# The first pair of heads of a fused attention and mixture kernel: one scaled rope table, keys before queries, queries in two column parts

## The chip, the cores and the metric

The kernel runs on one core of a Trainium2 chip. The metric is the device time of one execution in microseconds (us); less is better. A core has five engines with an instruction queue each: TensorE (PE, with weight loads shown apart as PEld), VectorE (DVE), ScalarE (ACT), GpSimd (POOL) and SyncE (SP), which here issues nearly all DMA transfers. An engine takes its instructions in the order in which they stand in its queue.

## What is computed

Three stages follow each other: attention over 4 batches of 8 heads, a gated layer over the positions, and a second attention with four experts. The change lies at the start of the first stage, whose reference is this:

```
q_rot, k_rot = rotate(q), rotate(k)            # rope: x1*cos - x2*sin, x1*sin + x2*cos
scores = q_rot @ k_rot.T / sqrt(64)            # per head, 576 x 576
attn = exp(scores - max); attn /= sum
out  = attn @ v                                # 576 x 64 per head
```

All of it is float32. Products that need full precision are made of parts: a value x is split into a high part, x rounded to the matmul format fp32r, and a low part, x minus the high part.

## The kernel before

The first stage goes through 16 pairs of heads. Class `Work` holds one pair. Head 0 of a pair lies on partitions 0 to 63 (slice `a`), head 1 on 64 to 127 (slice `c`), head dimension on the partitions, the 576 positions along the columns.

Preparation of a pair: `load` fetches tile t0 (queries) and t1 (keys), 576 KB each; each holds the values and the values with their halves swapped, so rope is two multiplications by the table `rp` and one addition. Then the rotated tiles are split and laid out: `q2` holds the high part of a head's queries on one half of the partitions and the low part on the other; `qz` holds the high part on one half and zeros on the other; `kh` holds the high part of the keys twice, `kl` (tile lo) the low part. In the trace the first pair's tiles stand as t, q, qz, kh and lo. A block of 128 query rows then takes four matmuls, two with q2 and kh, two with qz and kl: high x high, low x high and high x low. For all pairs but the first, `rope` runs on POOL, `parts` makes the high part on DVE and the low part on POOL, and `fill_q` and `fill_k` send them to their places by ten DMAs (144 KB each) within the chip. For the first pair, where all engines wait, `first` and `fill_direct` do it on DVE, ACT and POOL directly: queries first, then keys, whole 576 columns at a time. The table held in memory is scaled by 1/8; ACT makes a second copy times 8 for the keys.

A pair has nine blocks of 128 rows (four and a half of each head). Function `slot(k)` handles block k, and writes into the queues: on ACT the exponential of block k; on PE the scores of block k+1 and the transposes of block k-1; on DVE the row maximum (nmax) of block k+1; after each transposition a copy out of PSUM (g), on ACT for even blocks and on DVE for odd ones; in certain slots a gathering of leftover columns (DVE, e<-e) and the products with v (PE, ps_o). Scores have two PSUM buffers, so the scores of block k+1 wait for the exponential of block k-1. The order on PE, ACT, DVE and POOL within this stage is the written order (`keep_in_program_order`, switched on by `fixed`); on SP only some transfers are held in order, and a scheduler places the rest.

Within the first pair's slots the second pair is prepared: POOL multiplies its tiles by the table, adds those of the queries, and DVE adds those of the keys in slot 3. `parts(0)`, the queries, runs in slot 2, `parts(1)`, the keys, in slot 4.

Before the first pair's scores PE multiplies zeros (64 matmuls written, of several shapes). The zero halves of qz and the zero blocks of q2 are written by ACT at the very start, by `Pair.__init__`: per pair two blocks of q2, and 18 pieces of 64 columns of qz.

Of the kernel before, what the change touches and what calls it, by code (L numbers as in the profile page):

```python
# [43 lines left out]
def fused_kernel(ctx, tc, qk, v, w_in, w_out, w_sg, g_ln, b_sg, wqk, wvg, wo, rope, cst, out):  # L44
# [68 lines left out]
    class Pair:  # L113
# [5 lines left out]
        def __init__(self, one, x, some, turned=False):  # L119
            self.turned = turned  # L120
            self.q2 = one.tile([P, 2, 640], F32R, name=f"q2_{x}")
            self.qz = one.tile([P, 2, S], F32R, name=f"qz_{x}")
            z = slice(0, 64) if turned else slice(512, 576)
            for o in (self.q2[:, 0, 576:640], self.q2[:, 1, z]):
                ACT.activation(o, some[:, 0:64], AF.Copy, scale=0.0)
            for o in (self.qz[64:128, 0], self.qz[0:64, 1]):
                if not turned:
                    i = f(self.q2[0:64, 0, 576:640]).rearrange("p (o n) -> p o n", o=1).to_broadcast([64, 9, 64])
                    nc.sync.dma_start(f(o).rearrange("p (c n) -> p c n", c=9), i)
                    continue  # L130
                for c in range(0, S, 64):
                    ACT.activation(o[:, c:c + 64], some[0:64, 0:64], AF.Copy, scale=0.0)

        def block(self, j, i):

# [19 lines left out]
        def fill_q(self, qh, ql):  # L155
            q2, qz = self.q2, self.qz
            a, c = slice(0, 64), slice(64, 128)
            todo = [(q2[a, 0, 0:S], qh[a, :]), (qz[a, 0], qh[a, :])]
            if self.turned:
                todo += [(q2[c, 1, 64:640], qh[c, :]), (qz[c, 1], qh[c, :]), (q2[a, 1, 64:640], ql[c, :])]  # L160
            else:
                todo += [(q2[c, 1, 0:512], qh[c, 0:512]), (qz[c, 1, 64:S], qh[c, 0:512]), (q2[a, 1, 0:512], ql[c, 0:512])]
            todo.append((q2[c, 0, 0:S], ql[a, :]))
            if not self.turned:
                for o, i in ((q2[c, 1, 576:640], qh[c, 512:576]), (q2[a, 1, 576:640], ql[c, 512:576]),
                             (qz[c, 1, 0:64], qh[c, 512:576])):
# [4 lines left out]
        def fill_direct(self, pool, q, k, kl):  # L171

            q2, qz = self.q2, self.qz
            kh = self.kh = pool.tile([P, 2, S], F32R, tag="kh", name="kh", bufs=2)
            self.kl = kl
            a, c = slice(0, 64), slice(64, 128)

            def low(o, x, h):
                DVE.tensor_tensor(o, x, f(h), op=ALU.subtract)

            ACT.copy(q2[a, 0, 0:S], q[a, :])
            low(q2[c, 0, 0:S], q[a, :], q2[a, 0, 0:S])
            ACT.copy(kh[a, 0, :], k[a, :])
            DVE.tensor_copy(kh[c, 0, :], k[a, :])
            low(kl[a, :], k[a, :], kh[a, 0, :])
            ACT.copy(qz[a, 0], q[a, :])
            ACT.copy(q2[c, 1, 64:640], q[c, :])
            low(q2[a, 1, 64:640], q[c, :], q2[c, 1, 64:640])
            ACT.copy(kh[c, 1, :], k[c, :])
            DVE.tensor_copy(kh[a, 1, :], k[c, :])  # L190
            low(kl[c, :], k[c, :], kh[c, 1, :])
            nc.sync.dma_start(f(qz[c, 1]), f(q2[c, 1, 64:640]))

    def factor_out(wk, t, d):
        rr = wk.tile([9, P], F32, tag="rr", name="rr", bufs=1)
# [150 lines left out]
    with ExitStack() as st:  # L346
# [6 lines left out]
        ld2 = st.enter_context(tc.tile_pool(name="a_ld2", bufs=2))  # L353
        wk = st.enter_context(tc.tile_pool(name="a_wk", bufs=2))
        ptp = st.enter_context(tc.tile_pool(name="a_pt", bufs=1))
        rp = one.tile([P, 2, 2, S], F32, name="rp")
        zero = one.tile([P, P], F32, name="zero")
        DVE.memset(zero, 0.0)
        prs = [Pair(opd, x, zero, True) for x in range(2)]
# [17 lines left out]
        class Work:  # L377
# [3 lines left out]
            def load(self, n):  # L381
                self.n, self.b, self.p, self.pr = n, n // NP, n % NP, prs[n % 2]
                self.ts = []
                for x in range(2):
                    t = ld.tile([P, 2, S], F32, tag=f"t{x}", name=f"t{x}")
                    d = nc.sync.dma_start(t, qk[self.b, self.p, :, x])
                    if n == 1 and x == 0:
                        tc.keep_in_program_order(d)
                    if n == 0 and x == 0:
                        nc.sync.dma_start(rp[:, 0], rope)  # L390
                        for i in range(2):
                            ACT.activation(rp[:, 1, i], rp[:, 0, i], AF.Copy, scale=8.0)
                    self.ts.append(t)
                if n == 0:
                    nc.sync.dma_start(ident, cst[:, 0:P])

            def load_values(self):
                self.vt = ld.tile([P, NKB, 2, D], F32, tag="v", name="v", bufs=3)
                nc.sync.dma_start(self.vt, v[self.b, self.p])

            def first(self):

                ts = self.ts
                for x, i, eng in ((0, 0, DVE), (1, 1, POOL), (0, 1, DVE), (1, 0, DVE)):
                    eng.tensor_tensor(ts[x][:, i], ts[x][:, i], rp[:, x, i], op=ALU.mult)
                for t in ts:
                    DVE.tensor_tensor(t[:, 0], t[:, 0], t[:, 1], op=ALU.add)
                lo = ld2.tile([P, S], F32R, tag="lo1", name="lo1")
                self.pr.fill_direct(opd, ts[0][:, 0], ts[1][:, 0], lo)

            def rope(self, x, steps=(0, 1, 2), engine=POOL):
                t = self.ts[x]
                for i in steps:
                    if i < 2:
                        engine.tensor_tensor(t[:, i], t[:, i], rp[:, x, i], op=ALU.mult)
                    else:
                        engine.tensor_tensor(t[:, 0], t[:, 0], t[:, 1], op=ALU.add)

            def parts(self, x):
# [5 lines left out]
                POOL.tensor_tensor(lo, t[:, 0], f(hi), op=ALU.subtract)  # L425
# [101 lines left out]
        def slot(k):  # L527
# [97 lines left out]

        works = {0: Work(), 1: Work()}

        warm, warm2 = bank("l"), bank("o")
        zr = wk.tile([P, P], F32R, tag="e", name="zr", bufs=4)
        DVE.tensor_copy(zr, zero)  # L630
        for _ in range(16):
            PE.matmul(warm[:, 0:P], zero, zero, start=True, stop=True)
        for i in range(8):
            for h in (slice(0, 64), slice(64, 128)):
                PE.matmul(warm[h, 0:P], zero[:, 0:64], zero, start=True, stop=True)
        for i in range(8):
            for o, h in ((warm, slice(0, 64)), (warm2, slice(64, 128))):
                PE.matmul(o[:, 0:P], zero[h], zero[h], start=True, stop=True)
        for i in range(8):
            for o, h in ((warm, slice(0, 64)), (warm2, slice(64, 128))):  # L640
                PE.matmul(o[:, 0:P], zr[h], zr[h], start=True, stop=True)
        works[0].load(0)
        works[0].load_values()
        works[0].first()
        works[1].load(1)
        fixed[0] = True
        works[1].rope(0)
        works[1].load_values()
        works[1].rope(1, (0, 1))
        works[0].start()  # L650
        works[0].scores(0)
        works[0].maxima(0)
# [2 lines left out]
        for k in range(9 * B * NP + 7):  # L655
            n, x = divmod(k, 9)
            slot(k)
            if x in W_AT[4 if n == NP * B - 1 else min(n, 2 + n % 2)]:
                next(wload, None)
            if k == 9 * 4:  # L660
# [758 lines left out]
def layouts(q, k, v, moe_w_in, moe_g_ln, moe_w_sg, moe_b_sg, moe_w_out,  # L1419
# [16 lines left out]
    def chunks(w):  # L1436
# [60 lines left out]
```

## Time and profile before

| | us |
|---|---|
| median of 3 runs | 685.34 (685.2 to 685.43) |
| the profiled execution | 685.67 |
| its span, first to last instruction | 683.9 |
| PE busy | 669.8 (98%) |
| DVE busy | 453.8 (66%) |
| ACT busy | 428.7 (63%) |
| POOL busy | 343.5 (50%) |

The difference between the profiled execution's time and its span, 1.8 us, lies before the first and after the last instruction. Times in rows are us from the start of the span unless marked ns. Nearly all instructions carry line L58, that of a helper that records every operation, so rows are told apart by engine and tiles.

### The profile page before, as it was taken

The page shows a single profiled execution, that of the slowest core. Times are in us where ns is not written, and L with a number is a line of the kernel's source. Part 1 is how long each engine was busy: PE and PEld are TensorE (multiplying, and loading weights), DVE is VectorE, ACT ScalarE, POOL GpSimd, SP SyncE. Part 2 cuts the span into 40 slices and gives each one's busy share as a digit, 9 for nine tenths or more (in the row PEclk, how much of TensorE's full clock was granted, in tenths as well). Part 3 has the DMA queues.
Part 4 walks back from the last instruction along what each step waited for, and adds up shares of the span by engine and source line. Part 5 has one row for each costly group of instructions (what it writes and reads, how often), then busy time and mean ns, then how long its engine had stood idle before and what let it go on. Part 6 is the DMA issues. An engine that isn't in the chain of part 4 may idle for free.

```text
span 683.9 us, 13699 instructions
## 1 busy us (share of the span) xinstructions
PE 669.8 (98%) x4781; PEld 588.2 (86%) x4781; DVE 453.8 (66%) x1026; ACT 428.7 (63%) x1050; POOL 343.5 (50%) x333
## 2 busy tenths in 40 slices
PE   6999999999999999999999999999999999999997
PEld 6777777777777777799999999999999989999985
DVE  5777777777777867478964764664247666556673
ACT  6577776767777777564472473472156676666674
POOL 1886777778888861562446227206223443342320
PEclk9799999999999999999999999999999999999999
DMA  8588887888788762652465233055455364443522
GB/s 301 162 252 255 233 257 203 245 242 255 222 238 256 224 179 84 184 160 79 117 186 176 87 118 119 17 139 158 126 163 142 92 171 103 124 134 77 139 83 77
DMA packets 65538, 112.47 MB, mean 164 GB/s; under 512 B 20527, under 2 KB 25726, under 8 KB 65470
## 3 DMA queue, kind: packets, MB, share of 16 engines
q1 hardware_dynamic: 62734, 105.92, 53.6%
q10 hardware_dynamic: 2736, 5.68, 2.8%
q8 instruction: 38, 0.62, 0.4%
q14 instruction: 30, 0.25, 0.1%
HBM read 58.32 MB, written 18.98 MB: 113 GB/s over the span
## 4 chain that ended last, share of the span: by engine, by line
PE 89%; DVE 5%; ACT 4%; issue 1%; DMA 1%; SPq 0%; ACTq 0%; DVEq 0%
PE ps_S L58 48%; PE ps_o L58 17%; PE ps_t L58 14%; PE ps_f L58 5%; PE ps_s L58 3%; PE ps_l L58 2%; DVE nmax L58 1%; ACT qz L58 1%; ACT e L58 1%; DVE ga L58 1%; DMA x<-yd 1%; ACT ga L58 0%; ACT vh L58 0%; DVE g L58 0%; DVE q L58 0%
## 5 line engine op out<-in xcount | busy, mean ns | idle before, releaser
L58 ACT ACTIVATE e<-ps_S,nmax 128x576 f32<-128x576 f32 x144 | 108.0, 750 | 70.7 <-DVE nmax L58 70.1
L58 DVE TENSOR_REDUCE nmax<-ps_S 128x1 f32<-128x576 f32 x144 | 108.7, 755 | 58.0 <-PE ps_S L58 55.7
L58 PE MATMUL ps_t<-ident,e 128*128 128x128 f32 x776 | 122.0, 275 | 1.2 <-ACT e L58 0.7
L58 PEld LDWEIGHTS ps_t<-ident,e 128*128 128x128 f32 x776 | 95.8, 141 | 5.4 <-ACT e L58 1.3
L58 POOL TENSOR_TENSOR t<-t,rp 128x576 f32<-128x576 f32 x61 | 85.4, 1422 | 15.0 <-ACT rp L58 9.2
L58 PE MATMUL ps_S<-kh,q 128*128 128x288 f32 x352 | 88.0, 343 | 4.7 <-ACT kh L58 2.9
L58 PEld LDWEIGHTS ps_S<-kh,q 128*128 128x128 f32 x352 | 54.5, 193 | 33.3 <-issue 10.2
L58 PE MATMUL ps_o<-g,v 128*64 128x320 f32 (+1 forms) x512 | 76.2, 418 | 0.0
L58 POOL TENSOR_TENSOR lo<-t,hi 128x576 fp32r<-128x576 f32 x30 | 43.2, 1440 | 49.0 <-DVE hi L58 49.0
L58 PE MATMUL ps_S<-lo,qz 128*128 128x288 f32 x304 | 66.5, 300 | 1.4 <-DVE lo L58 1.4
L58 PEld LDWEIGHTS ps_o<-g,v 128*64 128x64 f32 x512 | 31.3, 136 | 24.2 <-issue 9.5
L58 PE MATMUL ps_S<-yh,w 128*128 128x288 f32 x256 | 51.8, 304 | 0.0
L58 PEld LDWEIGHTS ps_S<-lo,qz 128*128 128x128 f32 x304 | 49.8, 193 | 1.7 <-DVE lo L58 1.7
L58 ACT ACTIVATE e<-e,nmax 128x128 f32<-128x128 f32 (+4 forms) x72 | 42.2, 586 | 13.6 <-DVE nmax L58 13.4
L58 POOL TENSOR_TENSOR yl<-x,yh 128x640 fp32r<-128x640 f32 x16 | 26.0, 1630 | 47.7 <-ACT yh L58 47.7
L58 ACT COPY g<-ps_t 128x512 f32<-128x512 f32 x80 | 46.7, 584 | 3.0 <-PE ps_t L58 2.4
L58 DVE COPY g<-ps_t 128x512 f32<-128x512 f32 x64 | 43.6, 681 | 1.4 <-PE ps_t L58 1.3
L58 POOL TENSOR_TENSOR t<-t 128x576 f32<-128x576 f32 x29 | 41.4, 1427 | 2.3
L58 PEld LDWEIGHTS ps_S<-yh,w 128*128 128x128 f32 x256 | 38.7, 189 | 0.0
L58 ACT ACTIVATE ga<-ga 128x512 f32<-128x512 f32 (+1 forms) x34 | 22.3, 656 | 25.5 <-DVE ga L58 25.5
L58 PE MATMUL ps_S<-wsh,vh 128*128 128x288 f32 x160 | 34.6, 297 | 0.8 <-DVE u L58 0.5
L58 POOL TENSOR_TENSOR gxl<-u,gxh 128x576 fp32r<-128x576 f32 x16 | 22.8, 1434 | 24.0 <-ACT gxh L58 24.0
(290 smaller groups left out, 1751.3 us busy)
## 6 DMA issues: line engine op xcount, KB each, us to landing
t<-in_qk_dram SPq DMA_DIRECT2D x32, 576.0 KB
kh<-hi SPq DMA_DIRECT2D x92, 144.0 KB
q<-hi SPq DMA_DIRECT2D x38, 144.0 KB
qz<-hi SPq DMA_DIRECT2D x38, 144.0 KB
q<-lo SPq DMA_DIRECT2D x38, 144.0 KB
v<-in_v_dram SPq DMA_DIRECT2D x16, 320.0 KB
sa<-xr SPq DMA_DIRECT2D x16, 288.0 KB
xd<-sa SPq DMA_DIRECT2D x16, 288.0 KB
```

What stands on the lines that cost most here:

```text
L58: ins = op(*a, **k)
```

## The change

- `rp` holds one table, scaled by 1/sqrt(8) for queries and keys alike; ACT's copy of it goes. It is loaded in two transfers of 288 KB, one per factor.
- The first transfers are keys, table, queries (before: queries, table, keys). More transfers are held in written order on SP.
- `fill_direct` goes. `first` now ropes the keys on DVE, then the first 320 columns of the queries on DVE; ACT casts keys and these query columns; the low part of the second head's 320 columns is made on POOL. The other 256 columns are roped on POOL, and split in slot 1: two casts on ACT, two subtractions on DVE, and two DMAs of 64 KB for their copies in qz.
- The second pair: keys are multiplied first and split in slot 3 (before 4); queries are added on DVE in slot 4 and split in slot 5 (before 2), with their low part on DVE (before on POOL).
- `fill_q` sends the low part of the first head third instead of last, for all pairs.
- PE's zero matmuls before the scores become 18 of one shape, and three more stand behind the scores of slots 0, 1 and 2.
- The zeros of qz are written by two ACT instructions of 576 columns per pair instead of 18 of 64.

```diff
-                for c in range(0, S, 64):
-                    ACT.activation(o[:, c:c + 64], some[0:64, 0:64], AF.Copy, scale=0.0)
+                i = some[0:64, 0:64].rearrange("p (o n) -> p o n", o=1).to_broadcast([64, 9, 64])
+                ACT.activation(o.rearrange("p (c n) -> p c n", c=9), i, AF.Copy, scale=0.0)
...
-            todo = [(q2[a, 0, 0:S], qh[a, :]), (qz[a, 0], qh[a, :])]
+            todo = [(q2[a, 0, 0:S], qh[a, :]), (qz[a, 0], qh[a, :]), (q2[c, 0, 0:S], ql[a, :])]
...
-            todo.append((q2[c, 0, 0:S], ql[a, :]))
...
-        rp = one.tile([P, 2, 2, S], F32, name="rp")
+        rp = one.tile([P, 2, S], F32, name="rp")
...
+                for x in (1, 0) if n < 2 else (0, 1):
+                    d = nc.sync.dma_start(self.ts[x], qk[self.b, self.p, :, x])
+                    if n < 2:
                         tc.keep_in_program_order(d)
-                    if n == 0 and x == 0:
-                        nc.sync.dma_start(rp[:, 0], rope)
+                    if n == 0 and x == 1:
                         for i in range(2):
-                            ACT.activation(rp[:, 1, i], rp[:, 0, i], AF.Copy, scale=8.0)
+                            tc.keep_in_program_order(nc.sync.dma_start(rp[:, i], rope[:, i]))
...
+                full, s, u = slice(0, S), slice(0, 320), slice(320, S)
+                s1, u1 = slice(64, 384), slice(384, 640)
+                roped(k, full)
+                k = k[:, 0]
+                ACT.copy(kh[a, 0], k[a])
+                ACT.copy(kh[c, 0], k[a])
+                roped(w, s)
+                hi = one.tile([P, S], F32R, tag="hi1", name="hi1")
+                DVE.tensor_copy(hi, k)
+                low(kl, k, hi)
+                ACT.copy(q2[a, 0, s], q[a, s])
+                low(q2[c, 0, s], q[a, s], q2[a, 0, s])
+                ACT.copy(qz[a, 0, s], q[a, s])
+                ACT.copy(kh[c, 1], k[c])
+                ACT.copy(q2[c, 1, s1], q[c, s])
+                low(q2[a, 1, s1], q[c, s], q2[c, 1, s1], POOL)
+                ACT.copy(kh[a, 1], k[c])
+                ACT.copy(qz[c, 1, s], q[c, s])
+                roped(w, u, POOL)
+                yield
+                for o, i in ((q2[a, 0, u], q[a, u]), (q2[c, 1, u1], q[c, u])):
+                    ACT.copy(o, i)
+                low(q2[c, 0, u], q[a, u], q2[a, 0, u])
+                low(q2[a, 1, u1], q[c, u], q2[c, 1, u1])
+                for o, i in ((qz[a, 0, u], q2[a, 0, u]), (qz[c, 1, u], q2[c, 1, u1])):
+                    tc.keep_in_program_order(nc.sync.dma_start(f(o), f(i)))
+                yield
...
-                if x == (2 if n == 0 else 1):
-                    nx.parts(0)
-                if x == (4 if n == 0 else 3):
+                if n == 0 and x == 4:
+                    nx.rope(0, (2,), DVE)
+                if x == (5 if n == 0 else 1):
+                    nx.parts(0, POOL if n else DVE)
+                if x == 3:
                     nx.parts(1)
...
+            if k == 1:
+                next(start)
+            if k < 3:
+                warmed(3)
...
-    rope = np.stack([C / 8, Sg / 8], 1).astype(np.float32)
+    rope = (np.stack([C, Sg], 1).astype(np.float64) / np.sqrt(8.0)).astype(np.float32)
```

DVE at the start of the program, from the first multiplication to the last low part of the first pair. Before, t_266 is the queries and t_271 the keys:

```order
L58 TENSOR_TENSOR t_266<-t_266,rp 128x576 x2
L58 TENSOR_TENSOR t_266<-t_266 128x576
L58 TENSOR_TENSOR t_271<-t_271,rp 128x576
L58 TENSOR_TENSOR q_0_150<-t_266,q_0_150 64x576
L58 TENSOR_TENSOR t_271<-t_271 128x576
L58 TENSOR_TENSOR q_0_150<-t_266,q_0_150 64x576
L58 CAST kh<-t_271 64x576 x2
L58 TENSOR_TENSOR lo_282<-t_271,kh 64x576 x2
```

The same place after the change, where t_186 is the keys and t_185 the queries:

```order
L58 TENSOR_TENSOR t_186<-t_186,rp 128x576 x2
L58 TENSOR_TENSOR t_186<-t_186 128x576
L58 TENSOR_TENSOR t_185<-t_185,rp 128x320 x2
L58 TENSOR_TENSOR t_185<-t_185 128x320
L58 CAST hi_204<-t_186 128x576
L58 TENSOR_TENSOR lo_195<-t_186,hi_204 128x576
L58 TENSOR_TENSOR q_0_150<-t_185,q_0_150 64x320
```

The keys come first, their low part is one instruction on 128 partitions instead of two on 64, and the queries have 320 columns.

DVE in the first pair's slots, from the gathering of slot 1 to the second pair's last split. Before, hi_352 belongs to the second pair's queries, t_298 and hi_398 to its keys:

```order
L58 TENSOR_REDUCE e<-e 128x64
L58 TENSOR_REDUCE nmax<-ps_S 128x1
L58 COPY g_194<-ps_t 128x4x128
L58 CAST hi_352<-t_296 128x576
L58 TENSOR_REDUCE nmax<-ps_S 128x1
L58 TENSOR_REDUCE e<-e 128x64
L58 TENSOR_TENSOR t_298<-t_298 128x576
L58 TENSOR_REDUCE nmax<-ps_S 128x1
L58 COPY g_194<-ps_t 128x4x128
L58 CAST hi_398<-t_298 128x576
```

After it, t_219 and hi_304 are the second pair's keys, t_218, hi_358 and lo_359 its queries:

```order
L58 TENSOR_TENSOR q_0_150<-t_185,q_0_150 64x256 x2
L58 TENSOR_REDUCE nmax<-ps_S 128x1
L58 COPY g_162<-ps_t 128x4x128
L58 TENSOR_REDUCE nmax<-ps_S 128x1
L58 TENSOR_REDUCE e<-e 128x64
L58 TENSOR_TENSOR t_219<-t_219 128x576
L58 CAST hi_304<-t_219 128x576
L58 TENSOR_REDUCE nmax<-ps_S 128x1
L58 COPY g_162<-ps_t 128x4x128
L58 TENSOR_TENSOR t_218<-t_218 128x576
L58 TENSOR_REDUCE nmax<-ps_S 128x1
L58 TENSOR_REDUCE e<-e 128x64
```

Two subtractions of the first pair now stand in front of the fourth maximum, an addition and (right behind the last row shown) a cast and a subtraction of the second pair's queries behind it.

PE from the zero matmuls to the fourth block, after the change:

```order
L58 MATMUL ps_l<-zero 128x128 x18
L58 MATMUL ps_S<-kh,q_0_150 128x288 x2
L58 MATMUL ps_S<-lo_195,qz_151 128x288 x2
L58 MATMUL ps_S<-kh,q_0_150 128x288 x2
L58 MATMUL ps_S<-lo_195,qz_151 128x288 x2
L58 MATMUL ps_l<-zero 128x128 x3
L58 MATMUL ps_S<-kh,q_0_150 128x288 x2
L58 MATMUL ps_S<-lo_195,qz_151 128x288 x2
L58 MATMUL ps_t<-ident,e 128x128 x4
L58 MATMUL ps_l<-zero 128x128 x3
```

Before, the zero matmuls ended with 16 of tile zr, and from the first scores on the same rows stood without the groups of three.

## Rows read from the trace of the kernel before

**Rows 1.** The page: span, and busy time of each engine with its share

```profile
span 683.9 us, 13699 instructions
PE 669.8 (98%) x4781; PEld 588.2 (86%) x4781; DVE 453.8 (66%) x1026; ACT 428.7 (63%) x1050; POOL 343.5 (50%) x333
```

**Rows 2.** Windows: stretch, length, busy PE PEld DVE ACT POOL, PEclk, DMA share, GB/s

```profile
32.10:45.90 13.80, 13.80 (x104) 10.89 (x103) 10.16 (x21) 9.75 (x27) 12.40 (x10) 1.00 0.84 246
```

**Rows 3.** Windows, PE alone: stretch, length, PE busy, PEclk, DMA share, GB/s

```profile
3.00:10.00 7.00, 7.00 (x91) 1.00 1.02 405
11.00:13.00 2.00, 0.00 (x0) 1.00 0.65 233
14.00:15.00 1.00, 0.52 (x2) 0.58 0.68 147
18.00:24.00 6.00, 5.56 (x25) 0.50 0.16 68
24.00:25.00 1.00, 1.00 (x9) 0.80 0.00 0
```

**Rows 4.** Timeline, first pair's preparation: start, us, engine, operation [idle before <-releaser]

```profile
1.05 7.39 PE L58 MATMUL ps_l<-zero 128*128 128x128 f32 x65 [1.05 <-DVE zero L58]
5.60 2.86 ACT L58 ACTIVATE qz<-zero 64x64 fp32r<-64x64 f32 x18
5.93 1.43 DVE L58 TENSOR_TENSOR t<-t,rp 128x576 f32<-128x576 f32 x2 [4.68 <-DMA rp<-in_rope_dram]
9.51 0.66 ACT L58 CAST q<-t 64x576 fp32r<-64x576 f32 x1
13.91 0.60 PE L58 MATMUL ps_S<-kh,q 128*128 128x288 f32 x2 [2.94 <-ACT kh L58]
15.88 0.85 PE L58 MATMUL ps_S<-lo,qz 128*128 128x288 f32 x2 [1.36 <-DVE lo L58]
```

**Rows 5.** Timeline of the first pair's blocks, and the second pair's first two

```profile
18.44 0.85 PE L58 MATMUL ps_S<-kh,q 128*128 128x288 f32 x2 [0.75 <-ACT e L58]
22.47 0.69 DVE L58 COPY g<-ps_t 128x512 f32<-128x512 f32 x1
27.48 0.45 DVE L58 CAST hi<-t 128x576 fp32r<-128x576 f32 x1
32.12 0.53 PE L58 MATMUL ps_S<-kh,q 128*128 128x288 f32 x2
33.44 0.61 PE L58 MATMUL ps_S<-kh,q 128*128 128x288 f32 x2
```

**Rows 6.** Lines by form, of ACT until 100 us and of POOL: busy, mean ns

```profile
L58 ACT COPY xt<-ps_o 128x320 f32<-128x320 f32 x4 | 1.7, 419 | 0.0
L58 POOL TENSOR_TENSOR zl<-xt,zh 128x320 fp32r<-128x320 f32 x7 | 6.2, 882 | 0.6
```

**Rows 7.** Timeline, DVE beside POOL in the first pair

```profile
24.11 0.74 DVE L58 TENSOR_REDUCE nmax<-ps_S 128x1 f32<-128x576 f32 x1
24.26 1.41 POOL L58 TENSOR_TENSOR lo<-t,hi 128x576 fp32r<-128x576 f32 x1 [0.40 <-DVE hi L58]
24.77 0.20 DVE L58 TENSOR_REDUCE e<-e 128x64 f32<-128x64 f32 x1
24.90 1.39 DVE L58 TENSOR_TENSOR t<-t 128x576 f32<-128x576 f32 x1
```

**Rows 8.** Timeline, DVE beside POOL in the second stage

```profile
409.00 0.68 DVE L58 TENSOR_TENSOR vl<-gv,vh 128x512 fp32r<-128x512 f32 x1
...
409.34 1.64 POOL L58 TENSOR_TENSOR xl<-sa,xh 128x576 fp32r<-128x576 f32 x1 [0.51 <-DMA sa<-xr]
...
409.72 1.81 DVE L58 TENSOR_TENSOR vh<-g,vh 64x512 fp32r<-64x512 f32 x1
```

**Rows 9.** Timeline, SP: issue of the second pair's last four transfers

```profile
28.29 2.46 SPq L153 DMA_DIRECT2D kh<-hi  x4
```

**Rows 10.** DMA view from 24.2 to 32.8, in 40 slices of 0.215 us

```profile
GB/s 0 0 0 0 0 161 214 214 231 193 193 225 300 246 86 96 246 193 193 290 171 204 300 225 193 279 171 193 236 204 225 290 279 204 225 214 247 215 43 129
```

More of the change, by code (lines that the diff above doesn't have):

```diff
@@ L169, in fill_q @@
                 nc.sync.dma_start(f(o), f(i))
[L171 to L192, printed above, removed]
     def factor_out(wk, t, d):
@@ L384, in load @@
                 for x in range(2):
-                    t = ld.tile([P, 2, S], F32, tag=f"t{x}", name=f"t{x}")
-                    d = nc.sync.dma_start(t, qk[self.b, self.p, :, x])
-                    if n == 1 and x == 0:
+                    self.ts.append(ld.tile([P, 2, S], F32, tag=f"t{x}", name=f"t{x}"))
+                for x in (1, 0) if n < 2 else (0, 1):
+                    d = nc.sync.dma_start(self.ts[x], qk[self.b, self.p, :, x])
+                    if n < 2:
                         tc.keep_in_program_order(d)
-                    if n == 0 and x == 0:
-                        nc.sync.dma_start(rp[:, 0], rope)
+                    if n == 0 and x == 1:
@@ L391, in load @@
                         for i in range(2):
-                            ACT.activation(rp[:, 1, i], rp[:, 0, i], AF.Copy, scale=8.0)
-                    self.ts.append(t)
+                            tc.keep_in_program_order(nc.sync.dma_start(rp[:, i], rope[:, i]))
                 if n == 0:
-                    nc.sync.dma_start(ident, cst[:, 0:P])
+                    tc.keep_in_program_order(nc.sync.dma_start(ident, cst[:, 0:P]))
             def load_values(self):
                 self.vt = ld.tile([P, NKB, 2, D], F32, tag="v", name="v", bufs=3)
-                nc.sync.dma_start(self.vt, v[self.b, self.p])
+                tc.keep_in_program_order(nc.sync.dma_start(self.vt, v[self.b, self.p]))
@@ L401, in first @@
             def first(self):
[L403 to L409, printed above, removed]
+                pr, (q, k) = self.pr, self.ts
@@ new lines, in first, with roped @@
+                q2, qz, a, c = pr.q2, pr.qz, slice(0, 64), slice(64, 128)
+                kh = pr.kh = opd.tile([P, 2, S], F32R, tag="kh", name="kh", bufs=2)
+                kl = pr.kl = ld2.tile([P, S], F32R, tag="lo1", name="lo1")
+                def roped(t, s, engine=DVE):
+                    for i in range(2):
+                        engine.tensor_tensor(t[:, i, s], t[:, i, s], rp[:, i, s], op=ALU.mult)
+                    engine.tensor_tensor(t[:, 0, s], t[:, 0, s], t[:, 1, s], op=ALU.add)
@@ new lines, in low @@
+                def low(o, x, h, engine=DVE):
+                    engine.tensor_tensor(o, x, f(h), op=ALU.subtract)
+                q, w = q[:, 0], q
+                full, s, u = slice(0, S), slice(0, 320), slice(320, S)
[6 more added lines that the diff above has]
+                hi = one.tile([P, S], F32R, tag="hi1", name="hi1")
@@ L414, in rope, with parts @@
                     if i < 2:
-                        engine.tensor_tensor(t[:, i], t[:, i], rp[:, x, i], op=ALU.mult)
+                        engine.tensor_tensor(t[:, i], t[:, i], rp[:, i], op=ALU.mult)
                     else:
                         engine.tensor_tensor(t[:, 0], t[:, 0], t[:, 1], op=ALU.add)
-            def parts(self, x):
+            def parts(self, x, engine=POOL):
                 t = self.ts[x]
@@ L424, in parts @@
                 DVE.tensor_copy(hi, t[:, 0])
-                POOL.tensor_tensor(lo, t[:, 0], f(hi), op=ALU.subtract)
+                engine.tensor_tensor(lo, t[:, 0], f(hi), op=ALU.subtract)
                 if x == 0:
@@ L626, in fused_kernel, with warmed @@
         works = {0: Work(), 1: Work()}
[L628 to L641, printed above, removed]
+        warm = bank("l")
+        def warmed(n):
+            for _ in range(n):
+                PE.matmul(warm[:, 0:P], zero, zero, start=True, stop=True)
+        fixed[0] = True
+        warmed(18)
         works[0].load(0)
         works[0].load_values()
-        works[0].first()
+        start = works[0].first()
+        next(start)
         works[1].load(1)
-        fixed[0] = True
-        works[1].rope(0)
+        works[1].rope(1, (0, 1))
         works[1].load_values()
-        works[1].rope(1, (0, 1))
+        works[1].rope(0, (0, 1))
         works[0].start()
@@ L657, in fused_kernel @@
             slot(k)
+            if k == 1:
+                next(start)
+            if k < 3:
+                warmed(3)
             if x in W_AT[4 if n == NP * B - 1 else min(n, 2 + n % 2)]:
```

## The prediction

> **What bounds the kernel now.** I read the page first, then busy time by windows, then the timeline of the first 34 us. The page shows PE busy for 669.8 of 683.9 us [rows 1], so almost all of the span is PE working through its queue. From the second pair on this is exact: between 32.1 and 45.9 PE is busy for 13.80 of 13.80 us [rows 2]. A change in the first pair is therefore worth what it moves the moment from which PE never waits again. I take as that mark the scores of the second pair's second block, at 33.44 [rows 5]: up to there the change moves instructions, and behind it the queues of PE, ACT and DVE are the same.
>
> The other 14 us lie mostly ahead of that mark. PE multiplies zeros from 1.05 to 11, stands still from 11 to 13.9, does two score matmuls, and waits until 15.88 for the keys' low part [rows 3, 4]. Its clock follows: full from 11 to 13, a mean of 0.58 between 14 and 15, and 0.50 (1.2 GHz) from 18 to 24, where PE is busy for 5.56 of 6 us; then a mean of 0.80 between 24 and 25 [rows 3]. So it fell after PE had stood still, and came back only after it had worked nearly without gaps. Two score matmuls take 0.85 us at 1.2 GHz and 0.53 us at 2.4 [rows 5].
>
> **The preparation of the first pair.** In the trace the first multiplication starts at 5.93, when the table has landed behind the queries, 1,152 KB in all [rows 4]. Between 3 and 10 the DMA engines move 405 GB/s [rows 3], so 576 KB take 1.46 us and half a table 0.73. With the keys and the table's first half in front, DVE starts at 5.2, has its second factor at 5.93, and after two more operations of 0.72 us the rotated keys at 7.5 (0.72 is half of the 1.43 for two [rows 4]). The queries land one transfer later than the table, at 7.3 to 7.4. A 320-column operation with two inputs on DVE has no row. It costs between 0.20 (64 columns [rows 7]) and 0.72; I take 0.48, by a straight line between them, and three end at 8.9. The keys' high part costs 0.45 [rows 5], their low part 0.72, the queries' low part 0.48: DVE is through at 10.5. Both bounds move this by at most 1.1 us (four operations, 0.28 each).
>
> ACT first writes zeros. A wide copy has no row of its own; the nearest, a cast of 64x576, takes 0.66 [rows 4], so 2 of them replace 2.86 us per pair, ACT is free at 5.3 instead of 8.5, and even at twice the price the keys at 7.5 find it idle. Also the 1.2 us of copying the table go. Then come eight casts: four of 576 columns at 0.66, four of 320 at 0.42 (the row of the same width from PSUM [rows 6]). They follow each other with 0.1 of overlap, with a pause for the queries at 8.9, and end at 11.8. On POOL the second head's low part waits for the sixth cast, at 10.7, and takes 0.88 [rows 6], to 11.6. So the first block's scores start at 10.5 (before: 13.91, and 15.88 for the second half), the second's at 11.7.
>
> **The clock and the zero matmuls.** A zero matmul is two instructions; 65 of them filled 7.39 us [rows 4], so 36 end between 5 and 6.7. PE then stands still until 10.5, for 3.8 us or more where before it was 2.9, so I let the clock fall about when the scores begin. Scores at 1.2 GHz (1.1 to 1.2 us a block with its second half) and three zero matmuls (6 x 0.21 = 1.3 us at that clock) then keep PE busy almost without gap from 10.5 to 14.2. Before came to such a stretch only late, since PE was busy for just 0.52 of the microsecond from 14 to 15. I let the clock come back at 14.2; the bounds are that it never falls and that it takes as long as before, some ten microseconds. The third block's scores start at 14.0, 0.8 later than without the group of zeros in front; the other two groups cost 0.7 each at 2.4 GHz and stand where PE would wait for ACT or for the DMA of the last columns, so they cost nothing. That cover goes if the clock stays low.
>
> **From 14 to the mark it is DVE that sets the time.** The two subtractions of the first pair's last 256 columns (0.41 each, the same line) can start at 16.2, after the transposes and casts of slot 1. POOL is then multiplying the second pair's tiles without pause, 1.41 us an instruction [rows 7]. The trace shows what that does: an addition on DVE took 1.39 instead of 0.72 because POOL's subtraction from 24.26 to 25.67 had to end first [rows 7], while nmax, which reads PSUM, kept its 0.74. And at 409.00 [rows 8] the two take turns: DVE's subtraction makes POOL's take 1.64, and DVE's next one waits for all of that, 1.81 for an operation of 0.68. So of two in a row the second loses about 1.1. The second subtraction ends at 18.2 instead of 17.1, and the fourth block's maximum starts there. Behind it stand four maxima (0.66 apart, as from 24.11 to 24.77), two copies of 0.69, two gatherings (0.13), two additions (0.72), two casts (0.45) and the queries' subtraction (0.72): 7.0 us, overlaps of some 0.1 each taken off one and handovers put on the other. POOL is at work on the third pair's tiles by then, since their loads are long there, and the last cast and subtraction again wait, 0.3 and 1.0: the queries' low part is there at 26.7. In before POOL made it, beside DVE.
>
> The Trainium skill, page "SBUF — State Buffer", states in the passage with the single rule on ports that a two-input DVE instruction in SBUF and a reading POOL instruction exclude each other for a whole instruction, by order of issue. The trace agrees (1.81 against 0.68). Counted without this rule, the sum would come out 2.1 us earlier.
>
> Then SP sends six transfers for the queries. In the trace four issues take 2.46 us, 0.62 each [rows 9]; from 24.21, the issue of the first, bytes flow from 25.3 on and ten transfers are through at 32.3 to 32.7 [rows 10], that is 2.2 to 2.6 us behind the last one's issue at 30.1. With 2.4, the third lands at 29.2 and the sixth, issued at 28.7, at 31.1. The second pair's first two blocks start then, where PE with its transposes and products would have come by 27.6 and 29. For before the same walk gives 33.1 for the mark where the trace has 33.4, so I add the same 0.3: 31.4 against 33.4, a gain of 2.0 us.
>
> **The sum.** Start of scores 3.4 us earlier for the first half and 5.4 for the whole block; given back: about 0.8 by zero matmuls at the low clock, 2.1 by POOL and DVE in turns, and the wait for the queries' transfers. It stands against the profiled execution: 685.67 (span 683.9 and 1.8 around it) less 2.0 is 683.7. The median of the runs shown is 0.3 below that execution, so 683.3. The rest moves nothing on the mark: `fill_q`'s new order delays three transfers by one place in pairs that have some 10 us until they are needed, and the first load of the second stage's weights comes later but before its use in the second pair.
>
> **Rivals.**
> 1. The clock stays at 1.2 GHz beyond 14.2. Then the second and third groups of zeros take 1.3 instead of 0.7 each and stand ahead of scores that are ready. Until 17.6 that costs 1.4 at the mark, until 21 2.1. Time 684.7 to 685.4. For it: before it took ten microseconds to come back. Against: there PE had wide gaps at first, here it has none of that size. Chance 0.25.
> 2. The clock does not fall, or DVE and POOL miss each other at 16.2: 0.4 to 1.0 less, 682.3 to 682.9. For it: 0.1 us decides who gets the turn. Against: PE stands still for longer than before. Chance 0.15.
> 3. The queries' transfers replace the gain. They are queued behind the keys' four and a load of 576 KB (1.46 us), and a missed turn of DVE adds 1.4. Two such shifts together put the mark at 33.4 to 34: 685 to 685.8. Against: the load's place is 1 us ahead of the first query transfer. Chance 0.10.
> 4. Slower: the wait for the queries itself stops PE from 27.6 to 29.2 and again to 31, its work between them short, and the clock falls again with the second pair. Before's fall lasted from about 14.2 to 24.4; 10 us at half rate in a stretch where PE is never idle cost 5 us, half of that 2.5 if it returns sooner. 685.8 to 688.4, taken at 688. It decides if PE stands still as it did from 11 to 13.9. The Trainium skill, page "TensorE: Matmul & The Clock Gate", section "HAM oscillation — how this bites in real kernels", describes waits for transfers that put the clock back each time. Only the one fall of before shows it here. Against: the pieces of waiting are 1.6 and 0.7. Chance 0.08.
>
> **How the numbers follow.** The walk has 0.42. Its own range, from the bounds of the 320-column operations and of the landing, is 682.8 to 684.2. Rivals 1 to 3 widen it to 682.2 and 685.5, which leaves out rival 4 and the outer ends of the others, 0.2. A difference of 0.2%, 1.4 us, is about what a measurement of this kernel can tell from none, so faster means below 684.0. Most of the walk and rival 2 lie there, 0.54; the walk's late end, rival 1 and rival 3 are within, 0.38; above 686.7 most of rival 4, 0.08.
>
> **What would show it.** In the changed profile: the keys' multiplication at 5.2 and the first scores at 10.5, with two wide zero copies; PEclk at 0.50 only from about 11 to 14; DVE's subtraction on the queries' second part, and the second pair's, taking 1.4 to 1.8; the second pair's first scores near 29.5 with PE idle before them, and the second block's near 31.4. It is wrong if PEclk stays at 0.50 beyond 17, if PE reaches the second pair without waiting, or if the mark moves by 2 us and the end does not.

## The result, and the profile after

The changed kernel takes 692.35 us (median of 4 runs, 691.1 to 693.08), the kernel before 685.38 beside it: a ratio of 1.0102, 95% interval 1.009 to 1.0114. Forecast were 683.3 and a range of 682.2 to 685.5. The profiled execution took 693.08 us with a span of 691.3, 7.4 more than before [rows 1].

The page of the changed kernel: PE is busy for 1.6 us more [rows 1] and stands still for 5.8 us more (19.9 of 691.3 against 14.1 of 683.9).

```profile
span 691.3 us, 13548 instructions
PE 671.4 (97%) x4723; PEld 588.8 (85%) x4723; DVE 457.3 (66%) x1027; ACT 427.4 (62%) x1021; POOL 342.9 (50%) x334
```

The first pair's preparation came out nearly as walked through; compare [rows 4]. Timeline of the changed kernel (start us, us, engine, operation, idle before and its releaser):

```profile
2.44 1.38 ACT L58 ACTIVATE qz<-zero 64x576 fp32r<-64x576 f32 x2
...
5.57 1.43 DVE L58 TENSOR_TENSOR t<-t,rp 128x576 f32<-128x576 f32 x2 [4.57 <-DMA rp<-in_rope_dram]
...
8.96 0.49 DVE L58 TENSOR_TENSOR t<-t 128x320 f32<-128x320 f32 x1
...
11.19 0.54 PE L58 MATMUL ps_S<-kh,q 128*128 128x288 f32 x2 [3.67 <-DVE q L58]
...
17.32 3.23 DVE L58 TENSOR_TENSOR q<-t,q 64x256 fp32r<-64x256 f32 x2 [0.56 <-ACT q L58]
...
23.92 2.83 SPq L153 DMA_DIRECT2D kh<-hi  x4
...
26.85 0.53 SPq L363 DMA_DIRECT2D t<-in_qk_dram  x1
27.61 1.86 DVE L58 TENSOR_TENSOR lo<-t,hi 128x576 fp32r<-128x576 f32 x1
...
29.50 0.46 SPq L168 DMA_DIRECT2D q<-lo  x1
...
33.81 0.82 PE L58 MATMUL ps_S<-kh,q 128*128 128x288 f32 x2 [3.16 <-issue]
...
36.26 1.04 PE L58 MATMUL ps_S<-kh,q 128*128 128x288 f32 x2
```

First scores 2.7 us earlier than before; but the second pair's low part is made at 29.47 (forecast 26.7), its transfer is issued at 29.50, and PE, idle for 3.16 us, starts that pair at 33.81 instead of 32.12 [rows 5]. The view names no releaser for that wait ("issue"); by the semaphore steps of the trace the low part had landed at 33.61. The mark is at 36.26, 2.8 later than before. Windows of PE for the stretches of [rows 3] and two more (length, PE busy, PEclk, DMA share, GB/s):

```profile
11.00:13.00 2.00, 1.45 (x7) 0.87 0.32 126
14.00:15.00 1.00, 1.00 (x7) 0.50 1.01 387
16.00:18.00 2.00, 2.00 (x20) 1.00 0.04 14
18.00:24.00 6.00, 3.74 (x25) 0.89 0.44 123
24.00:25.00 1.00, 1.00 (x6) 0.50 0.00 0
30.00:34.00 4.00, 0.84 (x8) 0.87 1.04 253
34.00:40.00 6.00, 6.00 (x26) 0.52 0.90 301
```

The clock comes back after its first fall (1.00 from 16 on), and falls twice more: within 18 to 24, where PE had 3.74 us of work in 6 and its longest wait was 1.80 us (for an exponential), and at the end of the wait at 30 to 34. Between 34 and 40 PE is busy throughout at 0.52; before, that stretch had 1.00 [rows 2]. From here on one number follows a kernel: its lead or lag against the kernel before at the start of the same exponential on ACT. The lag is 4.4 us at 39, 4.9 at 66, 4.5 at 146, and 7.2 from 565 on. So 2.8 us more go in the third stage, where the change only touched the order of the query transfers. There the issue of four key transfers takes SP 3.35 us instead of 2.38. SP begins it 4.53 us later than before; the factor `r` that follows comes 6.19 us later (546.05 against 539.86), and PE waits 1.08 us where before it had no such wait. First the kernel before, then the changed one:

```profile
531.16 2.38 SPq L153 DMA_DIRECT2D kh<-hi  x4
...
539.86 0.74 POOL L58 TENSOR_TENSOR xt<-xt,r 128x256 f32<-128x256 f32 x1 [3.06 <-DMA r<-d]
```

```profile
535.69 3.35 SPq L153 DMA_DIRECT2D kh<-hi  x4
...
546.05 0.74 POOL L58 TENSOR_TENSOR xt<-xt,r 128x256 f32<-128x256 f32 x1 [4.73 <-DMA r<-d]
...
552.80 0.28 PE L58 MATMUL ps_o<-ident,rs 128*9 128x128 f32 x1 [1.08 <-POOL rs L58]
```

### The profile page after: what moved, and what is told of

It is laid out like the page before. It is cut to its first block, busy times and chain, and to the rows that moved or that the text cites. A ratio compares the mean times of both kernels' runs of the same rounds, so it can differ in the third digit from the quotient of the medians.

```text
span 691.3 us, 13548 instructions
## 1 busy us (share of the span) xinstructions
PE 671.4 (97%) x4723; PEld 588.8 (85%) x4723; DVE 457.3 (66%) x1027; ACT 427.4 (62%) x1021; POOL 342.9 (50%) x334
## 5 line engine op out<-in xcount | busy, mean ns | idle before, releaser
L58 PE MATMUL ps_S<-kh,q 128*128 128x288 f32 x352 | 88.3, 344 | 10.5 <-DVE q L58 4.1
L58 POOL TENSOR_TENSOR t<-t,rp 128x576 f32<-128x576 f32 (+1 forms) x62 | 86.1, 1411 | 0.1
L58 POOL TENSOR_TENSOR lo<-t,hi 128x576 fp32r<-128x576 f32 x29 | 41.8, 1441 | 57.8 <-DVE hi L58 55.7
L58 PEld LDWEIGHTS ps_o<-g,v 128*64 128x64 f32 x512 | 31.1, 136 | 24.4 <-issue 9.7
L58 ACT ACTIVATE e<-e,nmax 128x128 f32<-128x128 f32 (+4 forms) x72 | 42.2, 586 | 13.7 <-DVE nmax L58 13.3
L58 POOL TENSOR_TENSOR t<-t 128x576 f32<-128x576 f32 (+1 forms) x29 | 40.8, 1406 | 2.3
L58 ACT ACTIVATE ga<-ga 128x512 f32<-128x512 f32 (+1 forms) x34 | 22.3, 656 | 26.7 <-DVE ga L58 26.7
L58 PE MATMUL ps_S<-wsh,vh 128*128 128x288 f32 x160 | 34.6, 297 | 0.8 <-DVE u L58 0.5
```

Source lines behind the costliest of these rows:

```text
L58: ins = op(*a, **k)
```

## The experiments

Medians are in us, with the ratio to the kernel before and its 95% interval, or the lowest and highest time, in brackets; kernels of one group ran on one chip, and the kernel before had 685.08, 685.13, 685.03, 685.30 and 685.28 in the five groups.

**The order of the six query transfers.** e1 makes this edit in the kernel before; e2 takes it back in the changed one.

```
-  todo = [(q2[a, 0, 0:S], qh[a, :]), (qz[a, 0], qh[a, :])]
+  todo = [(q2[a, 0, 0:S], qh[a, :]), (qz[a, 0], qh[a, :]), (q2[c, 0, 0:S], ql[a, :])]
...
-  todo.append((q2[c, 0, 0:S], ql[a, :]))
```

> The kernel before, with only the new order of the six query transfers (the first head's low part third instead of last). Theory A, the order itself costs the 2.7 us that the changed kernel loses between 545 and 565 us of its span: 687.3 to 688.1 us. Theory B, that loss comes from where the slow DMA issues of SP happen to fall and the order costs at most the 0.6 us of one issue: 685.0 to 686.1 us.

> The changed kernel, with only the order of the query transfers put back. Theory A: 2.7 us below the changed kernel, 689.6 us. Theory B: 691.5 to 692.5 us, and its profile, if it loses time in the third stage, loses it at another place.

e1: 685.56 (ratio 1.0012, 1.0002 to 1.0022). e2: 693.89 (1.0124, 1.0109 to 1.0139), slower still and outside both ranges. Theory A falls, and theory B's range for e2 was missed: the order alone costs half a microsecond, and for the changed kernel it is a help, since its second pair waits for just that low part. With the order back PE's wait is 4.93 instead of 3.16 (e2):

```profile
35.66 0.82 PE L58 MATMUL ps_S<-kh,q 128*128 128x288 f32 x2 [4.93 <-DMA q<-lo]
```

**Zeros in the wait.** e3 puts 14 zero matmuls ahead of the second pair's first scores.

```
+  for _ in range(zeros):    # 14 at k == 8
+      PE.matmul(ps[:, 0, 0:P], zero, zero, start=True, stop=True)
```

> The changed kernel, with 14 zero matmuls more, right ahead of the second pair's first scores, where PE stands still for 3.16 us. Theory: of the 4.4 us lost by 39 us of the span, 1.7 are the wait for the queries and 2.7 the clock that falls because of it; the zeros take the clock's part away: 689.5 to 690.2 us, with no second fall of the clock at 33. Rival, the clock falls for another reason or the zeros only take the time that they save: 692 to 694 us.

690.39 (688.08 to 695.98). The median is just above the theory's range. In the profile, one of the quicker executions (688.97), the clock does not fall at 33 (window of PE) and the lag at 39 is 2.7 instead of 4.4:

```profile
30.00:34.00 4.00, 3.14 (x28) 1.00 1.02 278
```

Not all of this is the zeros' doing. Up to 30 us e3 has the changed kernel's instructions, and yet its clock was at 0.50 once, from 11.3 to 18.2, where the changed kernel's profile has 12.5 to 15.9 and again 22.7 to 26.1. So the falls differ between executions of the same instructions, and a single profile does not tell how many a kernel has. The lag at the end was 3.2: the third stage lost only 0.4, which no theory here had foreseen.

**The second pair prepared as before.** e4:

```
-  if n == 0 and x == 4: nx.rope(0, (2,), DVE)
-  if x == (5 if n == 0 else 1): nx.parts(0, POOL if n else DVE)
-  if x == 3: nx.parts(1)
+  if x == (2 if n == 0 else 1): nx.parts(0)
+  if x == (4 if n == 0 else 3): nx.parts(1)
...
-  works[1].rope(1, (0, 1))    # load_values() behind it
-  works[1].rope(0, (0, 1))
+  works[1].rope(0)            # load_values() behind it
+  works[1].rope(1, (0, 1))
```

> The changed kernel, with the second pair prepared as in the kernel before: queries ahead of keys on POOL, their split in slot 2 with the low part on POOL, the keys' split in slot 4. Theory: the second pair's preparation is what makes its first scores late (33.81 against 32.12), so they come at 31 to 32.5, PE waits for 0.5 to 1.5 us and the clock may hold: 687 to 689.5 us. Rival, the first pair's own work (POOL's share of the queries, the subtractions on DVE, the gaps of PE) sets the delay, and the order of the second pair does not matter: 691.5 to 693 us.

690.5 (688.75 to 694.53), in neither range. The first half of the theory holds: first scores of the second pair at 31.71, PE's wait for them 0.84 us, a lead of 0.4 us at 36. But the fourth pair waits, and the clock falls there (0.50 from 67.9 to 71.4). Timeline, then SP's waits from 50 to 62 of this kernel:

```profile
67.05 0.50 PE L58 MATMUL ps_S<-kh,q 128*128 128x288 f32 x2 [3.11 <-DMA kh<-hi]
```

```profile
SPq L168 <- DMA t<-in_qk_dram: 2.2, 1, 2.2
```

SP's query transfers stand behind the landing of an older load of 576 KB, and the keys' transfers behind them: these are issued at 61.00, in the kernel before at 58.33.

**The values' loads.** e5 is e4 with `load_values` tied to its place only for n < 2; e6 is the kernel before with it tied always; e12 (below) unties it in the changed kernel.

```
-  tc.keep_in_program_order(nc.sync.dma_start(self.vt, v[self.b, self.p]))
+  d = nc.sync.dma_start(self.vt, v[self.b, self.p])
+  if self.n < 2: tc.keep_in_program_order(d)
```

> As the kernel with the queries first again, and the values' loads are tied to their place in SP's queue in the first two pairs alone (the change ties all of them). Theory V: tying the values puts a load of 576 KB (t) ahead of the keys' four transfers from the third pair on, and that is the 3.11 us wait of the fourth pair's first scores at 64 us and the clock fall behind it; it goes: 685.3 to 686.8 us. Rival: the fourth pair's wait is a late echo of the second pair's: it stays, 689 to 690.5 us.

> The kernel before, with only the values' loads tied to their place in SP's queue. Theory V: the fourth pair's first scores, at 66 us, wait by 0.4 to 3.1 us, and the clock may fall once more: 685.5 to 689.2 us. Rival: no wait there, 684.8 to 685.4 us.

e5: 688.01 (1.0043, 1.0027 to 1.0058), between the two ranges, with waits of 1.42 (fourth pair) and 1.11 (fifth) for the keys left; e6: 685.85 (684.5 to 688.64), without a wait at 66 in its profile, which is the quickest of its twelve executions. Neither theory is right as it stands: untying gave 2.5 us from e4 to e5, tying cost the kernel before 0.7, and the fourth pair's wait has another cause too.

**The clock of the first pair.** e7 changes one number: `warmed(18)` to `warmed(36)`. e8 is e5 with 36.

> The changed kernel with 36 instead of 18 zero matmuls at the start, so that PE works until its first scores. Theory: the clock does not fall at 12, the first blocks come up to 1 us sooner, but VectorE, GpSimd and the transfers set when the second pair begins and PE stands still there as before: 691.3 to 692.8 us. Rival, the clock in the first pair is what the change loses: 689.3 to 690.5 us.

> Queries first again, values free, and 36 zero matmuls at the start: 0.3 to 1 us below the same kernel with 18 if the first pair's clock is worth something at the second pair's start, else the same; 684.3 to 686.5 us.

e7: 687.36 (686.45 to 688.33), 5.0 below the changed kernel. My theory falls and the rival was too small. Windows of PE in e7, the clock at 1.00 all through:

```profile
14.00:15.00 1.00, 0.96 (x7) 1.00 1.02 416
18.00:24.00 6.00, 4.48 (x30) 1.00 0.44 125
...
34.00:40.00 6.00, 6.00 (x46) 1.00 0.75 254
```

and its timeline: the low part is ready 1.4 us sooner, the wait for the second pair is still there, and the mark lies 0.35 ahead of before. The view puts the wait of 2.52 down to an exponential that had ended at 30.92; the low part landed at 31.09.

```profile
26.20 1.87 DVE L58 TENSOR_TENSOR lo<-t,hi 128x576 fp32r<-128x576 f32 x1
...
31.29 0.50 PE L58 MATMUL ps_S<-kh,q 128*128 128x288 f32 x2 [2.52 <-ACT e L58]
...
33.09 0.50 PE L58 MATMUL ps_S<-kh,q 128*128 128x288 f32 x2 [0.17 <-PE ps_o L58]
```

e8: 686.29, 1.7 below e5 where 0.3 to 1 was expected.

**What remains.** e9 is e8 with the query transfers' old order, so the first pair's part of the change alone. e10 also splits the last 256 columns at `k == 0` instead of `k == 1`, with 30 zeros. e11 is the kernel before with 13 zero matmuls more. e12 is e7 with the values free.

> The first pair's new preparation alone, with 36 zero matmuls: queries first, values free and the query transfers' old order for the pairs after it. Theory Q, the new order of the query transfers is what gives the early gain back later (it leaves a wait of 1.81 us at 143 us and one of 0.4 in the third stage): 684.0 to 685.2 us. Rival, any kernel that is early by a microsecond loses it to the transfers, whose queue is full: 685.5 to 686.6 us.

> The same, with the split of the last 256 query columns one slot earlier and 30 zero matmuls, which end about when the first scores can start. Theory: VectorE's two subtractions, 3.23 us in turns with GpSimd, are what holds the first pair back, and 1 us earlier they give 0.5 to 1.5 us at the second pair's start: 683.0 to 684.8 us. Rival: ACT then waits for GpSimd's columns ahead of the second exponential, and nothing is gained: 684.5 to 686 us.

> The kernel before, with 13 zero matmuls more at the start, so that PE works up to its first scores at 13.9. If the clock's fall from 14.2 to 24.4 costs the kernel before as much as the first fall costs the changed kernel: 681 to 683.5 us. Rival, there the fall lies beside waits for VectorE and GpSimd and costs nothing: 684.6 to 685.6 us.

> The changed kernel with 36 zero matmuls and the values free. Theory V, the tied values cost 0.7 us in the middle and up to 3.5 in some runs: 686.3 to 686.9 us, against 687.36 with them tied. Rival: 687.1 to 687.8 us.

e9: 684.6, ratio 0.9999 (0.999 to 1.0007), level with before; theory Q holds, the order costs 1.7 us here (686.29 less 684.6). Its timeline has the second pair as forecast:

```profile
30.47 0.53 PE L58 MATMUL ps_S<-kh,q 128*128 128x288 f32 x2
...
31.79 0.61 PE L58 MATMUL ps_S<-kh,q 128*128 128x288 f32 x2
```

e10: 684.82, nothing gained. e11: 685.77 (ratio 1.0013, 1.0004 to 1.0021): in its profile the clock is at 0.50 from 18.7 to 22.1 only, where before's is from 14.2 to 24.4, and nothing is gained by that. So the kernel before does not pay for the longer fall. e12: 687.19 against 687.36, with overlapping intervals: untying is worth 0.2 at most here, less than theory V had it.

**Order and clock apart.** e13 is e7 with the old transfer order, e14 is e9 with the change's 18 zeros.

> The changed kernel with 36 zero matmuls and the query transfers' old order. Theory Q, the new order costs 1.7 us wherever it stands: 685.3 to 686.2 us, against 687.36 with the new order. Rival, here the new order also helps, since the second pair's first scores wait for the low part, which the old order sends last (that cost 1.5 us with 18 zeros): 687.0 to 689 us.

> The first pair's new preparation alone (queries first, values free, old order behind it) with the change's own 18 zero matmuls. Theory, the clock's fall costs in any version that leaves PE idle ahead of its first scores: 1.5 to 2 us above the same with 36, 686.1 to 686.8 us. Rival, with the second pair on time the fall is hidden as in the kernel before: 684.3 to 685.3 us.

e13: 690.88, 3.5 above e7. The rival holds and goes beyond its range: with keys first the low part is the last thing to come, and sent last it makes PE wait longer:

```profile
32.43 0.82 PE L58 MATMUL ps_S<-kh,q 128*128 128x288 f32 x2 [4.28 <-DMA q<-lo]
```

e14: 687.64, 3.0 above e9 and above the theory's range, although its lead at 36 is the same (1.5 against 1.65). Between 146 us and the last exponential it loses 2.6 us, e9 0.6. The two differ in 18 zero matmuls, all ahead of 12 us. The key transfers of the third stage show the difference; SP in e14, then in e9:

```profile
530.01 3.10 SPq L153 DMA_DIRECT2D kh<-hi  x4
```

```profile
529.02 2.38 SPq L153 DMA_DIRECT2D kh<-hi  x4
```

The DMA view has a queue q8 of instruction loads, 38 of 16 KB in every kernel: one per some 250 of PE's instructions (9,446 matmuls and weight loads in e14). They follow PE's program and not the time: the 36th begins when PE has started 9,152 of its instructions in e14 and 9,120 in e9, although e9 has 72 more of them ahead of its first scores. The page of e14:

```profile
PE 667.7 (98%) x4723; PEld 585.1 (85%) x4723; DVE 454.0 (66%) x1025; ACT 426.6 (62%) x1021; POOL 345.2 (50%) x336
...
q8 instruction: 38, 0.62, 0.4%
```

One such load falls on the long issue in e14 (view of 530.5 to 532.5); in e9 none of this queue does from 526 to 532.

```profile
q8 instruction: 1, 0.02, 4.0%
```

Over all of e14's trace, 49 issues of SP overlap such a load: their mean is 0.92 us and 23 take over 0.85. Of the other 535 none does, and their mean is 0.51. The 18 zero matmuls are 72 instructions, over a quarter of the way from one load to the next.

**Loads or clock.** e15 (from e14) and e17 (from the changed kernel) make the 18 zero matmuls 256 columns wide, which fills the time of 36 and leaves PE's program as short as with 18; e16 and e18 add 18 matmuls of 4 columns.

```
+  PE.matmul(warm[:, 0:256]..., zero, zz, start=True, stop=True)      # e15, e17, in place of 128
+  PE.matmul(warm[:, 0:4], zero, zero[:, 0:4], start=True, stop=True)  # e16, e18, 18 times more
```

> The first pair's new preparation alone with 18 zero matmuls of 256 columns: as long as 36 of 128, but 18 matmuls fewer in PE's program. Theory L: what separates e9 (684.6) from e14 (687.64) is where PE's instruction loads (queue q8, 38 of 16 KB) fall among SP's DMA issues, and that hangs on the number of PE's instructions: 686.8 to 688.0 us, with long issues on the keys, the factor and the inputs of the third stage as in e14. Theory C, it is the clock, which is held here: 684.2 to 685.4 us.

> The first pair's new preparation alone with 18 zero matmuls of 128 columns and 18 of 4 columns: PE's program is as long as with 36, PE has little to do ahead of the first scores. Theory L: 684.3 to 685.4 us, as e9. Theory C: if the clock falls about 12 as in e14, 687 to 688 us.

> The changed kernel with its 18 zero matmuls made 256 columns wide. Both act in it: the clock holds in the first pair, which was worth 4.8 us up to the second pair in the trace of e7; by theory L the instruction loads stay where the changed kernel has them, and the third stage still loses 2 us: 688.8 to 690.2 us. Theory C: 687.0 to 687.9 us, as e7.

> The changed kernel with 18 zero matmuls of 4 columns behind its 18 of 128: the loads are moved as in e7, the clock is not helped by much. Theory L: the third stage loses 0.6 to 1 instead of 2.8 us, 689.8 to 691 us if the clock falls as before. Theory C: 691.6 to 692.8 us.

e15: 686.54 (685.98 to 687.52), 1.9 above e9: just below theory L's range, and 1.1 above all that theory C allows. The clock was held up to 23 there, but not throughout (window of PE), and in the profile 0.5 us against e9 had gone by 39 us:

```profile
25.00:27.00 2.00, 2.00 (x12) 0.53 0.91 213
```

Another 1.0 went at the fourth pair. An instruction load at 58.05 meets SP's issue of a value load, which takes 1.90 us; the keys behind it are issued at 60.06, and PE waits 0.95 us for them. e16: 686.18, in neither range: its small matmuls took PE until 13.3, so the first scores came 1.6 us late and the lead at 36 was 0.1; behind 146 us it lost 1.1. e17: 688.42 (687.82 to 692.91), between the two ranges, 1.1 above e7. Here the clock is at 1.00 all through (window of PE):

```profile
34.00:40.00 6.00, 6.00 (x47) 1.00 0.72 230
```

e18: 689.12, below both ranges and 3.2 below the changed kernel, with the clock at half from 10.7 to 17.5 and from 34.6 to 38.0 (33.0 to 39.8 in the changed kernel); behind 146 us it lost 1.2. What all profiles lose behind 146 us: with 18 matmuls 2.8 (changed), 1.1 (e2), 3.2 (e4), 3.7 (e5), 2.6 (e14), 1.7 (e15), 2.7 (e17); with 30 to 36 between 0.4 and 1.4 in nine. The two groups touch (e2), but SP's issues keep them apart: the twelve key transfers issued in the third stage up to 565 take SP 7.27 to 7.81 us in the seven profiles with 18 matmuls, and 6.61 to 6.64 in the other thirteen, the kernel before among them. So the place of the loads is worth 1 to 2 us, and theory C alone is out; that PE's loss follows from SP's longer issues is traced through the factor above, not tested apart.

## Why the prediction was wrong

The 7.0 us come apart like this: the clock 3.9 (692.35 to 688.42, e17), the place of PE's instruction loads 1.1 (to 687.36, e7), the second pair's preparation 1.1 (to 686.29, e8, values included), the transfers' order 1.7 (to 684.6, e9). Each kernel below changes one thing in the one above it.

| kernel | zero matmuls at the start | second pair | values' loads | transfers' order | median | ratio to before, 95% |
|---|---|---|---|---|---|---|
| changed | 18 | keys first | tied | new | 692.35 | 1.009 to 1.0114 |
| e17 | 18, twice as wide | keys first | tied | new | 688.42 | 1.0035 to 1.0078 |
| e7 | 36 | keys first | tied | new | 687.36 | 1.0024 to 1.0048 |
| e12 | 36 | keys first | free | new | 687.19 | 1.0026 to 1.0051 |
| e8 | 36 | queries first | free | new | 686.29 | 1.0007 to 1.0025 |
| e9 | 36 | queries first | free | old | 684.6 | 0.999 to 1.0007 |

e9 leaves 0.4 below before, which is not told from none. The intervals of e17 and e7 overlap, so the 1.1 for the loads rests on what the profiles lose behind 146 us more than on these two medians. The kernels ran on several chips, whose medians of the kernel before differ by up to 0.35. The steps interact (the order helps by 1.5 to 3.5 where the keys come first), so this is one way through them.

- **The preparation of the first pair** was right to 0.7 us: keys' multiplication 5.57 (5.2), first scores 11.19 (10.5), third block 14.53 (14.0); a 320-column operation 0.45 to 0.49 (0.48), a wide zero copy 0.69 (0.66). The zero matmuls ended at 7.5, not between 5 and 6.7, and PE stood still for 3.67 us.
- **"I let the clock come back at 14.2"**, priced at 0.8 us, is the step that failed first, and the largest: held at 1.00 (e17), the clock gives back 3.9 us. The first fall was sized about right (over by 16), but I took it to be the only one. It made the low part on DVE 1.4 us later (29.47 against 28.07 in e7), and two more falls followed. The page of the Trainium skill that the prediction cites on the clock, "TensorE: Matmul & The Clock Gate", section "HAM oscillation — how this bites in real kernels", describes falls that repeat, each behind a wait for a transfer. The trace agrees for the last fall, with 0.52 from 34 to 40 behind the wait for the queries; before the fall to 0.50 at 24 PE had waited for DVE and an exponential, 0.46 and 1.80 us.
- **"It is DVE that sets the time"** had the mechanism of the turns with POOL, and the size too small. The two subtractions took 3.23 us where the walk had 2.0; with the clock held they still took 2.9, and the low part came at 28.07 instead of 26.7 (e7).
- **The queries' transfers**, put at 2.5 us from the third's issue to the scores: 3.2 in e7 and 4.3 in the changed kernel, with a load of 576 KB issued 0.7 us ahead of the first. The walk's 2.4 us from issue to landing came from the kernel before, where no such load stood in front: there the first query transfer lands 2.3 us behind its issue (24.21 to 26.48), in the changed kernel 4.7 (27.60 to 32.30). This is what rival 3 named. It can set the time in place of DVE: in e17 the low part went out 1.0 us sooner than in e7 (27.12 against 28.09) and landed no sooner (31.13 against 31.09), the load of 576 KB having landed at 29.36 and 29.29.
- **Rival 4** was the right mechanism: the wait for the queries stops PE and the clock falls with the second pair. I gave it 0.08, since the pieces of waiting were 1.6 and 0.7 in the walk. They were 3.16 in one piece, because the two terms above were late by 2.8 and 1.8. Its price was too low as well, 688.4 at most.
- **"Behind it the queues of PE, ACT and DVE are the same"** is true and not enough. SP's queue is not the same, and PE's program is shorter by zero matmuls (4,723 matmul instructions against 4,781 [rows 1]), which shifts every later instruction load. **"`fill_q`'s new order delays three transfers by one place"**, put at nothing, cost 0.5 us in the kernel before and 1.7 between e8 and e9.
- **The sum** fails in its last link as well. With clock, transfers and second pair put right, the mark is 1.65 us ahead (forecast 2.0), and the time only 0.4. The profiled run of e9 kept 1.47 of it up to the last exponential, the median did not; where the other runs lose it stays open. So does all that makes the fourth pair wait when the queries come first, beyond the older load (e4) and the instruction load (e15).

## What to carry to other kernels

A wait of the bounding engine is to be priced with what its clock does afterwards, and a lead in an early stage only with the latest of the things that the next stage waits for: here the transfers, not the scores. Filling PE up to its first real work took one number and gave 5 us back, some 4 of them by the clock. When two versions differ after a point where their code is the same, compare the issue times of DMAs against the instruction loads before looking for a cause in the code.

## What the hardware showed that I had not expected

- A DMA issue of SP that meets an instruction load of PE takes longer: 0.92 us on the mean against 0.51 (e14). Where it falls is set by the number of PE's instructions, so that 18 zero matmuls at the start changed what the third stage loses by 1 to 2 us.
- A zero matmul of 4 columns is not cheaper than one of 128. In e16 (windows of PE) 33 instructions, most of them with 4 columns, fill 3.30 us at full clock, 0.10 each, and 18 fill 3.40 at half; the 128-column ones take 0.11 [rows 4].

```profile
6.70:10.00 3.30, 3.30 (x33) 1.00 1.04 414
10.00:13.40 3.40, 3.40 (x18) 0.50 1.04 416
```

- The length of a wait does not decide alone whether the clock falls: in e17 PE stood still for 3.54 us up to 31.33 and kept 1.00, in the changed kernel 3.16 us were followed by 0.52. The same instructions also fell at different times in different executions (e3 above). What decides is left open.

```profile
31.33 0.51 PE L58 MATMUL ps_S<-kh,q 128*128 128x288 f32 x2 [3.54 <-DMA qz<-hi]
```
